# A new order table for the first token block, four scalings moved from GpSimd to VectorE, weight fetches split in halves

## The chip, the core and the metric

The kernel runs on one core of a Trainium2 chip. TensorE (PE) multiplies matrices, VectorE (DVE), ScalarE (ACT) and GpSimd (POOL) work on tiles, SyncE (SP) issues most DMA transfers. Each engine takes its instructions in program order and waits on semaphores for the others. The metric is the device time of one execution in microseconds. Lower is better.

## The reference

Three stages follow one another on 3072 tokens (4 batches of 768) of 512 channels:

```python
state = gamma * state + k[t] (x) v[t];  y[t] = scale * q[t] @ state      # retention, 8 heads of 64, per batch
g = max(0.01 * h, h), h = x @ w_in;     x2 = g @ w_out                   # w_in 512x2048, w_out 2048x512
e = argmax(x2 @ w_gate);  out = gate * (relu(x2 @ w1[e]) @ w2[e])        # 8 experts, 512x1024 and 1024x512
```

`w_in` and `w_out` come as 64-bit floats, everything else as 32-bit floats. Products are made to nearly 32-bit precision out of three products of high and low parts (`hi`, `lo`).

## The kernel before

**Work.** Retention works in chunks of 128 tokens, the second stage in 8 blocks of 384 tokens (3 chunks). For a block, `mm1(i, f)` makes hidden slice f (0 to 15) from 12 matmuls; ScalarE and VectorE make g and its parts from it (`t` and `gh` on ScalarE, `max` and `gl` on VectorE); `mm2(i, f)` adds the slice's share to the block's output with 9 matmuls. The experts come last.

**Block 0** is unlike the others: while it runs, the weights of the second stage arrive and are converted, and chunks 0 to 5 of the retention are computed. Its order is written out by hand in the string `FIRST`. Every word is a step, and each engine meets its own steps in the order of the string:

- `w n` (line 129, SP): two DMAs of 512 KB, one for each half of weight fetch n, into a ring of raw buffers. Fetch n uses the buffers of fetch n-4, so each half waits until the `L` step of that half of fetch n-4 has read them. `w-1` and `w15` have one half.
- `D`, `A`, `H` (ScalarE, lines 160, 156, 179) and `B`, `C`, `L` (VectorE, lines 162, 167, 181) with `n.m`: conversion of half m of fetch n, in the order D and A, B, C, H, L. B and C put sign, exponent and mantissa together, C reading what B wrote; H makes the high part, L the low part. `n.0` is the slice of `w_in` that `mm1` of f = n+1 needs (`-1.0` for f = 0), `n.1` the slice of `w_out` that `mm2` of f = n needs.
- `kv n` loads chunk n; `q n` and `k n` (lines 217 and 223) multiply its queries and keys by decay factors, on VectorE or GpSimd; `S`, `mask`, `ya`, `yb`, `U`, `st` are its scores (PE), masking (VectorE), outputs (PE), state product (PE) and state; `xh n` (ScalarE) and `xl n` (VectorE) make the high and low part of its output, the input of `mm1`.
- `mm1_f` and `mm2_f` are the matmuls of slice f. `masks` builds the mask on GpSimd.

Before, GpSimd scales the queries of chunks 1 and 6 and on, and the keys of chunks 0, 1 and 6 and on; VectorE scales the queries of chunks 0 and 2 to 5 and the keys of chunks 2 to 4 (the queries of chunk 0 by way of its output). Chunk 5's keys are not scaled. Chunk 6, the first of block 2, is loaded at the word `st5` and scaled at the word `xl5`. Chunk 0's inputs are loaded in two halves, ahead of the first word of the string. `KW` adds a few matmuls on zeros behind some words.

Of the kernel before, what the change touches and what calls it, by code (L numbers as in the profile page):

```python
# [13 lines left out]
U32 = mybir.dt.uint32  # L14
# [5 lines left out]
B, H, S, D = 4, 8, 768, 64  # L20
# [30 lines left out]
S1 = 1  # L51
S2 = 0
# [2 lines left out]
AC = (4, 8, 12)  # L55
KW = {"S0": 2, "U0": 1, "S1": 2, "S2": 2}
FIRST = """
w-1 kv1 kv2 w0 w1 w2 S0 masks D-1.0 A-1.0 mask00 mask01 k0 B-1.0 yb0 C-1.0 U0 H-1.0 y0 st1 xh0 q1 xl0 L-1.0 w3 k1 S1 U1 mask10 mask11 ya1 st2 D0.0 yb1
q2 A0.0 k2 S2 D0.1 B0.0 xh1 C0.0 A0.1 mask20 D1.0 mask21 ya2 H0.0 xl1 A1.0 yb2 L0.0 D1.1 B0.1 A1.1 C0.1 xh2 B1.1 D2.0 H0.1 xl2 A2.0 C1.1 mm1_0 D2.1
B1.0 H1.1 C1.0 A2.1 B2.0 mm1_1 t0 L0.1 w4 kv3 H1.0 max0 A3.0 L1.1 U2 gh0 C2.0 A3.1 gl0 D4.0 L1.0 w5 t1 B2.1 H2.0 mm2_0 max1 D3.0 L2.0 gh1 D4.1 C2.1  # L60
A4.1 gl1 mm1_2 B3.0 H2.1 C3.0 D3.1 A4.0 L2.1 w6 kv4 mm2_1 t2 B3.1 H3.0 max2 D5.0 q3 gh2 L3.0 A5.0 mm1_3 gl2 D5.1 C3.1 st3 B4.0 C4.0 mm2_2 B5.0 H3.1
C5.0 t3 L3.1 w7 A6.0 mm1_4 max3 H5.0 B4.1 gh3 C4.1 D6.1 S3 gl3 H4.0 L5.0 H4.1 L4.0 t4 mm2_3 D6.0 mask31 A5.1 max4 D7.0 mask30 gh4 L4.1 w8 mm1_5 A7.1
gl4 A6.1 B5.1 A7.0 C5.1 t5 B7.0 mm2_4 H5.1 max5 A8.0 B6.1 gh5 L5.1 w9 D8.0 mm1_6 gl5 D8.1 C7.0 A8.1 q4 D9.0 B6.0 t6 mm2_5 H7.0 C6.0 A9.0 max6 L7.0
H6.0 ya3 k3 A9.1 yb3 L6.0 D9.1 gh6 C6.1 U3 kv5 D7.1 gl6 H6.1 B8.0 mm1_7 xh3 B7.1 st4 L6.1 w10 C8.0 C7.1 mm2_6 t7 xl3 H7.1 max7 H8.0 L7.1 w11 gh7 mm1_8
L8.0 gl7 B8.1 S4 A10.0 C8.1 t8 B9.0 D10.0 max8 H8.1 mask41 mm2_7 gh8 L8.1 w12 D10.1 C9.0 D11.0 A10.1 gl8 mm1_9 mask40 H9.0 B9.1 A11.1 L9.0 D11.1 C9.1
t9 mm2_8 A12.0 max9 H9.1 k4 gh9 B10.1 A12.1 gl9 mm1_10 D12.1 L9.1 w13 D12.0 C10.1 A13.0 B10.0 H10.1 mm2_9 C10.0 t10 B11.1 H10.0 C11.1 ya4 D13.0 max10
A11.0 yb4 L10.0 gh10 B11.0 A13.1 U4 C11.0 xh4 H11.1 gl10 mm1_11 q5 H11.0 L10.1 w14 w15 D13.1 st5 L11.0 L11.1 mm2_10 B12.0 t11 C12.0 A14.0 max11 H12.0
xl4 mm1_12 gh11 L12.0 D14.1 gl11 S5 A14.1 B13.0 t12 C13.0 D15.0 max12 A15.0 B12.1 mm2_11 gh12 C12.1 D14.0 gl12 H12.1 B13.1 mm1_13 C13.1 L12.1 H13.0
mask50 H13.1 L13.0 t13 mm2_12 max13 L13.1 gh13 mask51 gl13 mm1_14 B14.1 B14.0 t14 C14.0 mm2_13 max14 H14.0 C14.1 gh14 L14.0 H14.1 ya5 B15.0 yb5 L14.1
C15.0 xh5 gl14 mm1_15 H15.0 xl5 L15.0 t15 mm2_14 max15 gh15 gl15  # L70
"""


# [1 line left out]
def tile_retention_moe_moe(  # L75
# [12 lines left out]
    nc = tc.nc  # L88
# [26 lines left out]
    raws = {}  # L115

    def whalf(slot, h, dtype, nm):
        return wp.tile([128, 1024], dtype, tag=f"W{slot}{'ab'[h]}", name=nm)
# [7 lines left out]
    def pieces(n):  # L126
        return [(0, n + 1), (1, n)] if 0 <= n < 15 else [(0, 0)] if n < 0 else [(1, 15)]

    def w_fetch(n):
        if n in (-1, 15):  # L130
            t = [whalf(12, 0, U32, "raw") if n < 0 else stg.tile([128, 1024], U32, tag="stg", name="stg")]
        else:
            s, h = 12 + 2 * (n % 2 == 0), int(n % 4 in (1, 2))
            t = [whalf(s + x, h, U32, "raw") for x in range(2)]
        raws[n] = t
        for x in range(len(t)):
            nc.sync.dma_start(out=t[x][:, :512 * (2 if wide else 1)], in_=w[n + 1, :, x].bitcast(U32))

    def conv(o, n, m):
        x, f = pieces(n)[m]  # L140
        conv_op(o, n, m, x, f)
# [53 lines left out]
    def attn_load(n):  # L195
        b, cc = divmod(n, 2 * NC)
        if n == 2:

            t = [whalf(8, h, F32, "kv") for h in range(2)]
            parts = [t[x // 2][:, x % 2 * 512:x % 2 * 512 + 512] for x in range(4)]  # L200
            for h in range(2):
                nc.sync.dma_start(out=t[h], in_=qkv[b, cc, :, h * 1024:(h + 1) * 1024])
        else:
            t = at.tile([128, 2048], F32, tag="kv", name="kv")
            parts = [t[:, x * 512:x * 512 + 512] for x in range(4)]
            if n == 0:
                nc.sync.dma_start(out=t[:, :1024], in_=qkv[b, cc, :, :1024])
                nc.scalar.dma_start(out=small, in_=c_m[:, :200])
                nc.scalar.dma_start(out=qd, in_=c_m[:, 200:])
                nc.sync.dma_start(out=t[:, 1024:], in_=qkv[b, cc, :, 1024:])  # L210
            else:
                nc.sync.dma_start(out=t, in_=qkv[b, cc])
        loads[n] = parts

    def attn_q(n):
        q = loads[n][0]
        (nc.vector if n in (0, 2, 3, 4, 5) else nc.gpsimd).tensor_mul(q, q, qd)

    def attn_k(n):
        cc = n % (2 * NC)  # L220
        if cc < 5:
            k = loads[n][2].rearrange("p (g d) -> p g d", d=64)
            (nc.vector if n in (2, 3, 4) else nc.gpsimd).tensor_mul(k, k, kd[:, cc].unsqueeze(2).to_broadcast([128, 8, 64]))

    def pairs():
        return [(j, h, slice(64 * h, 64 * h + 64), slice(j * 128 + 64 * h, j * 128 + 64 * h + 64), slice(j * 128, (j + 1) * 128))
# [557 lines left out]
    raw = {}  # L784
# [8 lines left out]
    for x in ORDER:  # L793
        k = sum(y[0] == x for y in items)
# [408 lines left out]
    with tc.manual_schedule():  # L1203
# [22 lines left out]
        def first(word, o, n, m):  # L1226
            if o in ("A", "B", "C", "D", "H", "L"):
                conv(o, n, m)
            elif o == "w":
                w_fetch(n)  # L1230
            elif o == "kv":
                attn_load(n)
            elif o == "masks":
                masks()
            elif o == "q":
                attn_q(n)
            elif o == "k":
                attn_k(n)
            elif o == "S":
                banks[n] = attn_scores(n, tag_s.get(n, ("m0", "m1")))  # L1240
            elif o == "mask":
                ams[n, m] = attn_mask(n, banks[n][m], m)
            elif o == "ya":
                ys[n] = attn_yq(n, tag_y.get(n, ("m0", "m1")))
            elif o == "yb":
                ys[n] = attn_y(n, [ams[n, h] for h in range(2)], ys.get(n))
            elif o == "y":
                y0 = early["y"].rearrange("p (j t) -> p j t", j=4)
                nc.vector.tensor_mul(y0[:, :2], ys[n][0][0][:, :2], qd.rearrange("p (j t) -> p j t", j=4)[:, :2])
                nc.vector.tensor_mul(y0[:, 2:], ys[n][0][0][:, 2:], early["qy"])  # L1250
                ys[n] = [(y0, slice(0, 4))]
            elif o == "U":
                attn_U(n)
            elif o == "st":
                attn_state(n)
            elif o == "xh":
                attn_xh(n, ys[n])
            elif o == "xl":
                attn_xl(n, ys[n])
            elif o == "mm1":  # L1260
                banks["h", n] = mm1(0, n)
            elif o == "t":
                h = banks["h", n]
                gs[n] = gp.tile([128, TB], F32, tag="t", bufs=1, name="t")
                nc.scalar.activation(out=gs[n], in_=h, func=ACTF.Copy, scale=0.01)
            elif o == "max":
                nc.vector.tensor_max(gs[n], gs[n], banks["h", n])
            elif o == "gh":
                ghi = gp.tile([128, TB], F32R, tag="gh", name="gh")
                nc.scalar.copy(out=ghi, in_=gs[n])  # L1270
                gs[n] = gs[n], ghi
            elif o == "gl":
                act_b(0, n, *gs[n])
# [174 lines left out]
```

## Time and profile before

| | |
|---|---|
| device time, median of 3 runs | 988.24 us (987.54 to 989.04) |
| profiled execution | 989.41 us, its span 987.4 us |
| PE busy | 968.1 us, 98% |
| VectorE busy | 526.9 us, 53% |
| ScalarE busy | 422.4 us, 43% |
| GpSimd busy | 157.6 us, 16% |

The span runs from the first to the last instruction in the trace. Times in the rows are microseconds from its start. A timeline row gives start and duration, engine and line, what is written from what, and in brackets how long the engine had been idle and what it had waited for. A start-to-start distance of two rows of one engine is the price of the first in a full queue; durations of neighbours overlap a little.

### The profile page before, as it was taken

How to read it: one execution, taken by the hardware profiler on the slowest of the kernel's cores; microseconds unless marked ns; L12 is line 12 of the kernel's file. 1: busy time of each engine (PE TensorE's matmuls, PEld its weight loads, DVE VectorE, ACT ScalarE, POOL GpSimd, SP SyncE). 2: the span in 40 equal slices, each digit the busy share in tenths (PEclk: the TensorE clock that was granted, in tenths of full speed). 3: DMA queues.
4: the chain of work that ended last, by engine and by line, in shares of the span. 5: the costliest groups of instructions: out<-in, count | busy, mean ns of one | idle time of the engine just before them, and what ended most of it. 6: DMA issues, size and time to landing. Idle time of an engine off the chain costs nothing.

```text
span 987.4 us, 16775 instructions
## 1 busy us (share of the span) xinstructions
PE 968.1 (98%) x6513; PEld 843.4 (85%) x6513; DVE 526.9 (53%) x1092; ACT 422.4 (43%) x771; POOL 157.6 (16%) x131
## 2 busy tenths in 40 slices
PE   7998999999999999999999999999999999999996
PEld 6887888988888888888888888888988887887985
DVE  5999544434443443444444357555754655755741
ACT  4986332223222232222222233533655656655741
POOL 2001021021012010111102000633211321222111
PEclk9999999999999999999999999999999999999999
DMA  8773222323323213213413012312037968967600
GB/s 342 271 252 133 85 59 60 91 60 59 88 63 59 60 47 104 60 33 79 99 33 76 18 33 90 103 33 76 27 104 283 292 256 326 318 221 253 205 24 31
DMA packets 75105, 121.06 MB, mean 123 GB/s; under 512 B 36108, under 2 KB 36494, under 8 KB 72208
## 3 DMA queue, kind: packets, MB, share of 16 engines
q1 hardware_dynamic: 70352, 105.96, 34.5%
q0 software_dynamic: 4384, 13.65, 4.0%
q8 instruction: 51, 0.84, 0.4%
q10 hardware_dynamic: 288, 0.36, 0.1%
q14 instruction: 30, 0.25, 0.1%
HBM read 117.06 MB, written 13.25 MB: 132 GB/s over the span
## 4 chain that ended last, share of the span: by engine, by line
PE 73%; issue 10%; DMA 6%; DVE 5%; ACT 3%; POOL 2%; POOLq 0%; ACTq 0%; SPq 0%
PE x L371 25%; PE h L331 24%; PE m L932 6%; PE m L957 6%; DMA out_dram<-mq,sidx 3%; DMA raw<-in_w_dram 3%; PE ay L237 2%; PE y L281 2%; PE m L988 1%; PE m L1016 1%; PE y L272 1%; PE xt L893 1%; ACT raw L160 1%; PE m L1029 1%; DVE wl L181 1%
## 5 line engine op out<-in xcount | busy, mean ns | idle before, releaser
L350 DVE TENSOR_TENSOR t<-t,h 128x384 f32<-128x384 f32 x111 | 61.2, 552 | 158.3 <-ACT t L349 158.3
L862 DVE TENSOR_TENSOR wu<-raw,wu 128x1024 fp32r<-128x1024 f32 x96 | 114.0, 1222 | 47.6 <-ACT wu L861 46.4
L932 PE MATMUL m<-xe,wu 128*128 128x256 f32 x1056 | 137.6, 284 | 0.1
L932 PEld LDWEIGHTS m<-xe,wu 128*128 128x128 f32 x1056 | 132.3, 191 | 3.2 <-issue 0.5
L358 DVE TENSOR_TENSOR gl<-t,gh 128x384 fp32r<-128x384 f32 x127 | 80.4, 633 | 94.2 <-ACT gh L351 93.5
L349 ACT ACTIVATE t<-h 128x384 f32<-128x384 f32 x111 | 54.4, 490 | 155.9 <-PE h L331 125.6
L371 PE MATMUL x<-wh,gl 128*128 128x512 f32 x288 | 116.1, 403 | 1.8 <-DVE gl L358 1.8
L371 PE MATMUL x<-wl,gh 128*128 128x512 f32 x288 | 113.2, 393 | 1.4 <-DVE wl L181 1.4
L371 PE MATMUL x<-wh,gh 128*128 128x512 f32 x288 | 112.7, 391 | 0.0
L351 ACT CAST gh<-t 128x384 fp32r<-128x384 f32 x111 | 57.0, 514 | 128.0 <-PE x L371 71.2
L957 PE MATMUL m<-wu,gh 128*128 128x512 f32 x352 | 109.2, 391 | 0.0
L861 ACT CAST wu<-raw 128x1024 fp32r<-128x1024 f32 x104 | 104.5, 1047 | 3.0 <-DMA raw<-in_w_dram 3.0
L331 PE MATMUL h<-xh,wl 128*128 128x384 f32 x384 | 85.9, 345 | 0.8 <-ACT xh L292 0.7
L478 POOL TENSOR_TENSOR xr<-xr,b 128x512 f32<-128x512 f32 x18 | 20.9, 1164 | 398.4 <-DVE gl L358 231.8
L331 PE MATMUL h<-xl,wh 128*128 128x384 f32 x384 | 82.7, 336 | 0.2 <-DVE xl L298 0.2
L331 PE MATMUL h<-xh,wh 128*128 128x384 f32 x384 | 82.1, 334 | 0.0
L957 PEld LDWEIGHTS m<-wu,gh 128*128 128x128 f32 x352 | 66.3, 188 | 12.4
L331 PEld LDWEIGHTS h<-xh,wl 128*128 128x128 f32 x384 | 66.5, 188 | 5.1 <-ACT xh L292 1.0
L957 PE MATMUL m<-wu,gl 128*128 128x512 f32 x176 | 70.2, 399 | 0.4 <-DVE gl L944 0.3
L331 PEld LDWEIGHTS h<-xl,wh 128*128 128x128 f32 x384 | 68.9, 188 | 0.5 <-DVE xl L298 0.5
L331 PEld LDWEIGHTS h<-xh,wh 128*128 128x128 f32 x384 | 67.9, 188 | 0.0
L371 PEld LDWEIGHTS x<-wh,gl 128*128 128x128 f32 x288 | 54.0, 188 | 14.7 <-DVE gl L358 2.5
(267 smaller groups left out, 1462.3 us busy)
## 6 DMA issues: line engine op xcount, KB each, us to landing
raw<-in_w_dram SPq DMA_DIRECT2D x159, 512.0 KB
kv<-in_qkv_dram SPq DMA_DIRECT2D x22, 1024.0 KB
x2d<-xr SPq DMA_DIRECT2D x24, 256.0 KB
kv<-in_qkv_dram SPq DMA_DIRECT2D x4, 512.0 KB
t<-b SPq DMA_TRANSPOSE x36
stg<-in_w_dram SPq DMA_DIRECT2D x1, 512.0 KB
mq<-in_cm_dram ACTq DMA_DIRECT2D x1, 256.0 KB
kv<-x2d,gidx POOLq DMA_INDIRECT x16, 4.4
```

Of the source, the lines that this page charges most:

```text
L237: nc.tensor.matmul(banks[h][:, js], kt[r, js], q[r, js], start=True, stop=True, skip_group_check=True)
L331: nc.tensor.matmul(h, wcols(a, fc * 512 + k * 128, 128), x[:, k, :], start=(n == 0), stop=(n == 11))
L349: nc.scalar.activation(out=t, in_=h, func=ACTF.Copy, scale=0.01)
L350: nc.vector.tensor_max(g, t, h)
L351: nc.scalar.copy(out=ghi, in_=g)
L358: nc.vector.tensor_sub(glo, g, ghi.bitcast(F32))
L371: nc.tensor.matmul(x2ps[i][t], a[:, ts], wcols(w, f % 4 * 512), start=(f == 0 and n == 0), stop=(f == 15 and n == 2))
L478: (nc.gpsimd if S1 else nc.vector).tensor_sub(x, x, b1)
L861: nc.scalar.copy(out=hi, in_=src)
L862: (nc.gpsimd if g == 0 else nc.vector).tensor_sub(lo, src, hi.bitcast(F32))
L932: nc.tensor.matmul(bank, wp_[k // 2][a][:, c:c + 128], x[:, k, :], start=(n == 0), stop=(n == 11))
L957: nc.tensor.matmul(m2ps[2 * q + h], a[:, ts], w[:, fs], start=(f == 0 and n == 0), stop=(f == 7 and n == 2))
```

## The change

Three things are in the diff. The string `FIRST` is a new order of the same steps, with the fetches 4 to 14 (apart from 8) written as two words, one for each half, and `w_fetch` issues the halves that the word names. The queries and keys of chunks 1 and 6 are scaled by VectorE. Chunk 6 is scaled at the word `gl15`, the last of the string, and no longer at `xl5`. The description of the change also names the first weights as moved ahead of the second half of chunk 0's inputs; no line of the diff does this, `attn_load(0)` still issues both halves ahead of the string.

```diff
@@ -55,19 +55,19 @@
 AC = (4, 8, 12)
 KW = {"S0": 2, "U0": 1, "S1": 2, "S2": 2}
 FIRST = """
-w-1 kv1 kv2 w0 w1 w2 S0 masks D-1.0 A-1.0 mask00 mask01 k0 B-1.0 yb0 C-1.0 U0 H-1.0 y0 st1 xh0 q1 xl0 L-1.0 w3 k1 S1 U1 mask10 mask11 ya1 st2 D0.0 yb1
-q2 A0.0 k2 S2 D0.1 B0.0 xh1 C0.0 A0.1 mask20 D1.0 mask21 ya2 H0.0 xl1 A1.0 yb2 L0.0 D1.1 B0.1 A1.1 C0.1 xh2 B1.1 D2.0 H0.1 xl2 A2.0 C1.1 mm1_0 D2.1
-B1.0 H1.1 C1.0 A2.1 B2.0 mm1_1 t0 L0.1 w4 kv3 H1.0 max0 A3.0 L1.1 U2 gh0 C2.0 A3.1 gl0 D4.0 L1.0 w5 t1 B2.1 H2.0 mm2_0 max1 D3.0 L2.0 gh1 D4.1 C2.1
-A4.1 gl1 mm1_2 B3.0 H2.1 C3.0 D3.1 A4.0 L2.1 w6 kv4 mm2_1 t2 B3.1 H3.0 max2 D5.0 q3 gh2 L3.0 A5.0 mm1_3 gl2 D5.1 C3.1 st3 B4.0 C4.0 mm2_2 B5.0 H3.1
-C5.0 t3 L3.1 w7 A6.0 mm1_4 max3 H5.0 B4.1 gh3 C4.1 D6.1 S3 gl3 H4.0 L5.0 H4.1 L4.0 t4 mm2_3 D6.0 mask31 A5.1 max4 D7.0 mask30 gh4 L4.1 w8 mm1_5 A7.1
-gl4 A6.1 B5.1 A7.0 C5.1 t5 B7.0 mm2_4 H5.1 max5 A8.0 B6.1 gh5 L5.1 w9 D8.0 mm1_6 gl5 D8.1 C7.0 A8.1 q4 D9.0 B6.0 t6 mm2_5 H7.0 C6.0 A9.0 max6 L7.0
-H6.0 ya3 k3 A9.1 yb3 L6.0 D9.1 gh6 C6.1 U3 kv5 D7.1 gl6 H6.1 B8.0 mm1_7 xh3 B7.1 st4 L6.1 w10 C8.0 C7.1 mm2_6 t7 xl3 H7.1 max7 H8.0 L7.1 w11 gh7 mm1_8
-L8.0 gl7 B8.1 S4 A10.0 C8.1 t8 B9.0 D10.0 max8 H8.1 mask41 mm2_7 gh8 L8.1 w12 D10.1 C9.0 D11.0 A10.1 gl8 mm1_9 mask40 H9.0 B9.1 A11.1 L9.0 D11.1 C9.1
-t9 mm2_8 A12.0 max9 H9.1 k4 gh9 B10.1 A12.1 gl9 mm1_10 D12.1 L9.1 w13 D12.0 C10.1 A13.0 B10.0 H10.1 mm2_9 C10.0 t10 B11.1 H10.0 C11.1 ya4 D13.0 max10
-A11.0 yb4 L10.0 gh10 B11.0 A13.1 U4 C11.0 xh4 H11.1 gl10 mm1_11 q5 H11.0 L10.1 w14 w15 D13.1 st5 L11.0 L11.1 mm2_10 B12.0 t11 C12.0 A14.0 max11 H12.0
-xl4 mm1_12 gh11 L12.0 D14.1 gl11 S5 A14.1 B13.0 t12 C13.0 D15.0 max12 A15.0 B12.1 mm2_11 gh12 C12.1 D14.0 gl12 H12.1 B13.1 mm1_13 C13.1 L12.1 H13.0
-mask50 H13.1 L13.0 t13 mm2_12 max13 L13.1 gh13 mask51 gl13 mm1_14 B14.1 B14.0 t14 C14.0 mm2_13 max14 H14.0 C14.1 gh14 L14.0 H14.1 ya5 B15.0 yb5 L14.1
-C15.0 xh5 gl14 mm1_15 H15.0 xl5 L15.0 t15 mm2_14 max15 gh15 gl15
+w-1 kv1 kv2 w0 w1 w2 S0 masks D-1.0 A-1.0 mask01 k0 mask00 yb0 B-1.0 C-1.0 U0 y0 H-1.0 q1 xh0 st1 S1 L-1.0 w3 k1 mask11 U1 mask10 D0.0 st2 ya1 q2 A0.0
+yb1 xl0 D0.1 B0.0 A0.1 S2 k2 xh1 C0.0 D1.0 mask20 A1.0 mask21 H0.0 D1.1 xl1 ya2 A1.1 L0.0 w4.0 yb2 A2.0 B0.1 D2.0 B1.0 xh2 C0.1 A2.1 xl2 H0.1 C1.0 mm1_0
+D3.0 L0.1 w4.1 kv3 H1.0 B1.1 A3.1 L1.0 w5.0 t0 mm1_1 A3.0 max0 D4.0 C1.1 gh0 B2.0 U2 H1.1 gl0 D2.1 C2.0 t1 L1.1 w5.1 H2.0 mm2_0 max1 A4.1 B2.1 gh1 B3.0
+D4.1 C2.1 D3.1 mm1_2 A4.0 gl1 q3 H2.1 C3.0 t2 D5.0 mm2_1 L2.0 w6.0 H3.0 max2 A5.1 L2.1 w6.1 kv4 gh2 L3.0 w7.0 D5.1 mm1_3 gl2 st3 B3.1 A5.0 B4.1 t3 C3.1
+mm2_2 D6.0 C4.1 A6.0 max3 H4.1 B4.0 gh3 mm1_4 L4.1 D6.1 gl3 H3.1 C4.0 A6.1 S3 L3.1 w7.1 H4.0 B5.0 t4 A7.0 L4.0 w8 mm2_3 D7.0 max4 C5.0 gh4 mask30 H5.0
+gl4 mm1_5 L5.0 w9.0 D7.1 mask31 A7.1 B5.1 t5 D8.0 mm2_4 B6.0 A8.0 max5 D8.1 C5.1 gh5 C6.0 H5.1 mm1_6 gl5 D9.0 L5.1 w9.1 A9.0 k3 A8.1 B6.1 mm2_5 H6.0 q4
+t6 L6.0 ya3 C6.1 yb3 max6 H6.1 B7.0 gh6 U3 kv5 w10.0 L6.1 w10.1 A9.1 xh3 gl6 mm1_7 C7.0 st4 xl3 H7.0 B7.1 D9.1 L7.0 w11.0 t7 mm2_6 B8.0 max7 C8.0 gh7
+C7.1 mm1_8 H8.0 gl7 H7.1 L8.0 A10.0 S4 L7.1 w11.1 w12.0 t8 D10.0 B8.1 A10.1 B9.0 mm2_7 D10.1 C8.1 D11.0 C9.0 H8.1 max8 H9.0 mask41 mm1_9 gh8 L8.1 w12.1
+D11.1 gl8 A11.0 L9.0 w13.0 t9 B9.1 A11.1 mm2_8 max9 D12.0 C9.1 gh9 mask40 A12.0 H9.1 gl9 mm1_10 B10.1 A12.1 L9.1 w13.1 D12.1 C10.1 t10 D13.0 mm2_9 B10.0
+H10.1 B11.0 A13.0 C10.0 ya4 C11.0 yb4 H10.0 k4 A13.1 L10.0 w14.0 U4 xh4 max10 D13.1 L10.1 w14.1 w15 gh10 mm1_11 B11.1 st5 gl10 C11.1 t11 q5 H11.0 mm2_10
+B13.1 H11.1 L11.0 D14.0 xl4 A14.0 D14.1 max11 mm1_12 B13.0 A14.1 gh11 B12.0 D15.0 S5 gl11 A15.0 C12.0 t12 L11.1 H12.0 max12 mm2_11 L12.0 gh12 B12.1 gl12
+C12.1 mm1_13 C13.0 H12.1 C13.1 t13 L12.1 H13.0 max13 mm2_12 H13.1 L13.0 gh13 L13.1 gl13 B14.1 mm1_14 mask50 mask51 t14 B14.0 mm2_13 max14 C14.0 gh14
+C14.1 ya5 H14.0 gl14 yb5 H14.1 L14.0 L14.1 xh5 B15.0 mm1_15 xl5 C15.0 t15 H15.0 mm2_14 max15 L15.0 gh15 gl15
 """
 
 
@@ -126,14 +126,16 @@
     def pieces(n):
         return [(0, n + 1), (1, n)] if 0 <= n < 15 else [(0, 0)] if n < 0 else [(1, 15)]
 
-    def w_fetch(n):
+    def w_fetch(n, halves):
         if n in (-1, 15):
             t = [whalf(12, 0, U32, "raw") if n < 0 else stg.tile([128, 1024], U32, tag="stg", name="stg")]
         else:
             s, h = 12 + 2 * (n % 2 == 0), int(n % 4 in (1, 2))
-            t = [whalf(s + x, h, U32, "raw") for x in range(2)]
+            t = raws.get(n, [None] * 2)
+            for x in halves:
+                t[x] = whalf(s + x, h, U32, "raw")
         raws[n] = t
-        for x in range(len(t)):
+        for x in halves[:len(t)]:
             nc.sync.dma_start(out=t[x][:, :512 * (2 if wide else 1)], in_=w[n + 1, :, x].bitcast(U32))
 
     def conv(o, n, m):
@@ -214,13 +216,13 @@
 
     def attn_q(n):
         q = loads[n][0]
-        (nc.vector if n in (0, 2, 3, 4, 5) else nc.gpsimd).tensor_mul(q, q, qd)
+        (nc.vector if n in (0, 1, 2, 3, 4, 5, 6) else nc.gpsimd).tensor_mul(q, q, qd)
 
     def attn_k(n):
         cc = n % (2 * NC)
         if cc < 5:
             k = loads[n][2].rearrange("p (g d) -> p g d", d=64)
-            (nc.vector if n in (2, 3, 4) else nc.gpsimd).tensor_mul(k, k, kd[:, cc].unsqueeze(2).to_broadcast([128, 8, 64]))
+            (nc.vector if n in (1, 2, 3, 4, 6) else nc.gpsimd).tensor_mul(k, k, kd[:, cc].unsqueeze(2).to_broadcast([128, 8, 64]))
 
     def pairs():
         return [(j, h, slice(64 * h, 64 * h + 64), slice(j * 128 + 64 * h, j * 128 + 64 * h + 64), slice(j * 128, (j + 1) * 128))
@@ -1227,7 +1229,7 @@
             if o in ("A", "B", "C", "D", "H", "L"):
                 conv(o, n, m)
             elif o == "w":
-                w_fetch(n)
+                w_fetch(n, [m] if "." in word else [0, 1])
             elif o == "kv":
                 attn_load(n)
             elif o == "masks":
@@ -1280,6 +1282,7 @@
                 attn_load(6)
             elif word == "xl5":
                 attn_load(7)
+            elif word == "gl15":
                 attn_q(6)
                 attn_k(6)
             elif word == "mm1_8":
```

## Rows read from the trace of the kernel before

**Rows 1.** The page, busy time and share of the span by engine
```profile
PE 968.1 (98%) x6513; PEld 843.4 (85%) x6513; DVE 526.9 (53%) x1092; ACT 422.4 (43%) x771; POOL 157.6 (16%) x131
```

**Rows 2.** Stretches: length, then busy us of each engine, granted clock, DMA share, GB/s
```profile
30.00:40.00 10.00, 9.36 (x46) 8.45 (x47) 9.93 (x19) 9.77 (x22) 0.00 (x0) 1.00 1.00 366
...
90.00:100.00 10.00, 7.90 (x33) 6.92 (x32) 9.70 (x14) 2.83 (x6) 3.23 (x2) 0.83 0.00 0
```

**Rows 3.** PE's waits, 0 to 130 us: total, times, longest
```profile
PE x L371 <- DVE w L181: 2.1, 1, 2.1
...
PE x L371 <- DVE gl L358: 1.5, 2, 1.2
PE x L371 <- DVE wl L181: 1.4, 2, 0.8
```

**Rows 4.** The chain that ended last, 48 to 111 us: start, duration, what
```profile
48.26 4.75 DMA raw<-in_w_dram
...
82.46 3.83 DMA raw<-in_w_dram
...
94.56 3.10 PE x L371 x8
97.66 2.69 PE h L331 x12
...
106.36 2.08 PE x L371 x9
108.44 2.10 PE h L331 x12
```

**Rows 5.** A finer stretch, columns as in rows 2
```profile
97.00:98.00 1.00, 1.00 (x4) 0.88 (x3) 1.00 (x3) 0.00 (x0) 0.00 (x0) 0.50 0.00 0
```

**Rows 6.** VectorE's timeline where its queue is full
```profile
24.56 0.75 DVE L298 TENSOR_TENSOR xl<-y,xh 128x256 fp32r<-128x256 f32 x2
...
25.83 0.69 DVE L162 SCALAR_TENSOR_TENSOR raw<-raw 128x512 uint32<-128x512 uint32 x1
26.55 0.69 DVE L167 SCALAR_TENSOR_TENSOR raw<-raw 128x512 uint32<-128x512 uint32 x1
...
27.76 0.68 DVE L181 TENSOR_TENSOR wl<-raw,wh 128x512 fp32r<-128x512 f32 x1
28.36 0.55 DVE L1267 TENSOR_TENSOR t<-t,h 128x384 f32<-128x384 f32 x1
28.83 0.69 DVE L181 TENSOR_TENSOR wl<-raw,wh 128x512 fp32r<-128x512 f32 x1
```

**Rows 7.** VectorE's timeline, three instructions beside GpSimd's
```profile
14.14 1.37 DVE L298 TENSOR_TENSOR xl<-early,xh 128x512 fp32r<-128x512 f32 x1 [0.35 <-ACT xh L292]
...
91.39 1.66 DVE L167 SCALAR_TENSOR_TENSOR val<-raw 128x512 uint32<-128x512 uint32 x1
92.98 1.53 DVE L181 TENSOR_TENSOR w<-val,w 128x512 fp32r<-128x512 f32 x1
```

**Rows 8.** GpSimd's timeline, 0 to 150 us
```profile
13.92 1.04 POOL L223 TENSOR_TENSOR kv<-kv,mq 128x512 f32<-128x512 f32 x1
...
90.72 1.78 POOL L217 TENSOR_TENSOR kv<-kv,mq 128x512 f32<-128x512 f32 x1 [75.76 <-DMA kv<-in_qkv_dram]
92.47 1.49 POOL L223 TENSOR_TENSOR kv<-kv,mq 128x512 f32<-128x512 f32 x1
```

**Rows 9.** ScalarE's timeline, from fetch 1's landing to chunk 2's output
```profile
20.67 0.68 ACT L160 ACTIVATE raw<-raw 128x512 uint32<-128x512 uint8 x1 [0.59 <-DMA raw<-in_w_dram]
...
23.51 0.62 ACT L292 CAST xh<-y 128x256 fp32r<-128x256 f32 x2
```

**Rows 10.** PE's timeline, the first matmuls of block 0
```profile
23.91 0.97 PE L331 MATMUL h<-xh,wl 128*128 128x384 f32 x4 [0.72 <-ACT xh L292]
```

**Rows 11.** ScalarE's waits, 24 to 95 us: total, times, longest
```profile
ACT raw L156 <- DMA raw<-in_w_dram: 1.4, 2, 0.9
ACT raw L160 <- DMA raw<-in_w_dram: 1.0, 2, 0.7
```

## Prediction

> **What bounds the kernel now.** I read the page first: PE is busy for 98% of the span [rows 1]. From the table of stretches onwards, what is left to win lies almost wholly in block 0: VectorE is busy 9.93 us of the ten from 30 to 40, ScalarE 9.77 [rows 2], and PE waits for VectorE there. The list of PE's waits names three sources of size, 2.1 + 1.5 + 1.4 = 5.0 us, all on VectorE's `L` or `gl` [rows 3]. The longest is one wait of 2.1 us, and behind it the chain view holds PE alone: from 94.56 on, nothing but matmuls, so what PE gains in block 0 it keeps to the end. The 8 matmuls behind that wait take 3.10 us where 9 take 2.08 later, the next `mm1` takes 2.69 against 2.10 [rows 4]. The granted clock explains it: 0.50 from 97 to 98, that is 1.2 instead of 2.4 GHz, after the wait [rows 5]. Loss by the clock: 3.10 - 8/9 x 2.08 = 1.25, and 0.59, together 1.84 us.
>
> The timeline of VectorE shows why the wait is there. The instruction that PE waits for is `L12.1`, at 92.98; it takes 1.53 us, the `C13.1` ahead of it 1.66 [rows 7], where such instructions have 0.69 and 0.68 [rows 6]. In just this stretch GpSimd scales chunk 6, from 90.72 to 94 [rows 8]. The two instructions lost (1.66 - 0.69) + (1.53 - 0.68) = 1.82 us.
>
> **VectorE's queue, part by part.** I count what VectorE does from the end of `xl2` (next start 24.56 + 0.67 = 25.23) to the end of `L12.1` (94.43 by start-to-start price). Both strings have 113 instructions there, the same kinds: 85 on 128x512 tiles, 26 `max` and `gl`, 2 `xl`. Prices from start to start: 0.60 for a 128x512 one (27.76 to 28.36), 0.47 for `max` or `gl` (28.36 to 28.83), 0.67 for `xl` (2 instructions) [rows 6]. With 0.605 and 0.467 before rounding, 51.4 + 12.1 + 1.3 = 64.8 us.
>
> *Pairs.* A `C` right behind its own `B` starts 0.72 us after it (25.83 to 26.55), 0.12 more than the 0.60 [rows 6]. In the old string 15 such pairs stand in this stretch, in the new none: 15 x 0.12 = 1.8 us are removed. The Trainium skill (VectorE: DVE Perf Modes, section "The DRAIN you can't avoid") states that VectorE's chained instructions take as long with a semaphore after each as with one at the end. By that the pairs would cost nothing and the sum would come out 1.8 us later; the row differs, and I go by the row.
>
> *GpSimd's neighbours.* Scaling chunk 6 at `gl15` on VectorE takes 1.82 us out of this stretch. It adds 2 x 0.60 us behind the last `gl`, where PE has two `mm1` of 2.10 us of block 1 to do before it needs anything later from VectorE: hidden. If that cover failed it would cost 1.2 us.
>
> *The rest.* 94.43 - 25.23 = 69.20; 69.20 - 64.8 - 1.8 - 1.82 = 0.8 us are short waits and rounding. For the new string I take twice that, 1.6, since in the first 20 us of the stretch, up to `gl4`, ScalarE has 40 steps in both strings, and VectorE 40 in the old but 38 in the new: ScalarE, hardly less full there [rows 2], loses the little lead it had, and each will wait for the other more. Bounds: 0.8, and what the ring rival below gives. New length 64.8 + 1.6 = 66.4 us.
>
> **The start.** `q1` and `k1` join VectorE's queue, 2 x 0.60 = 1.2 us; `xl0`, which took 1.37 us beside GpSimd's `k1` [rows 7, 8], falls to 0.68, and two pairs are parted, 0.24. VectorE thus comes to `xl2` at 24.56 + 1.2 - 0.69 - 0.24 = 24.8. The scores of chunk 1 can start earlier, but that gains nothing: ScalarE waits until 20.67 for the landing of fetch 1 all the same, which the change does not move [rows 9]. From that landing to `xh2` the old string has five ScalarE steps, (23.51 - 20.67) / 5 = 0.57 us each; the new has seven (`A2.0` and `D2.0` now stand ahead of `xh2`). So `xh2` starts at 20.67 + 7 x 0.57 = 24.65, 1.1 later. PE's first `mm1` began 0.40 after `xh2` [rows 9, 10]: now 25.05. `xl2` can't start sooner either: its end moves from 25.23 to 25.05 + 0.67 = 25.72. This is a cost of 0.5 us for VectorE and 1.1 for PE.
>
> The split fetches cost SP the same DMAs, two per fetch; each half already waited for its own `L` alone, so the words only change what stands between on SP's queue (`kv3`, `kv4`, `kv5`): nothing, with the ring rival as the bound. Weights ahead of chunk 0's second half are not in the diff: nothing; were they, the landing of fetch 1, behind the same bytes, would still set 20.67.
>
> **The sum.** `L12.1` is done at 25.72 + 66.4 = 92.1, against 94.43. PE then had 108.44 - 94.56 = 13.88 us to the end of block 0, 1.84 of them lost to the clock: 12.04 without. With the same 0.13 between: 92.1 + 0.13 + 12.04 = 104.3, against 108.44. Gain 4.1 us, of which VectorE's queue brings 2.3 and the clock 1.8. The best case is PE alone: 108.44 - 23.91 - 5.0 - 1.84 = 77.7 us of work [rows 3, 4, 10], from 25.05 to 102.75, a gain of 5.7. The span of 987.4 becomes 983.3, and 2.0 us lie around it (989.41 in the profiled execution, 1.2 above the median). On the median: 988.24 - 4.1 = 984.1 us.
>
> **The rivals.**
>
> *The clock falls all the same.* By the sum PE, 1.1 late and without stalls on the way, would come to `mm2_12` at 94.56 - 2.1 - (1.5 + 1.4) + 1.1 = 90.7 and find `L12.1` 1.4 us away; and ahead of the first `mm1` the wait of 0.72 grows to some 1.9. For it: after 2.1 us the clock did fall. Against it: after the wait of 1.2 us near 30 [rows 3] it stayed at 1.00 [rows 2], and VectorE's lateness will come in several shorter waits (the `L11.1` of the `mm2` before is due by the same prices only 0.4 us less late). The Trainium skill (TensorE: Matmul & The Clock Gate, section "HAM oscillation — how this bites in real kernels") has matmuls behind a long wait for data start at the lower clock; the trace agrees at 97 us. Price 1.84 again: gain 2.3, 985.9 us.
>
> *The pairs cost nothing*, because what follows a parted pair waits as long for something else. Gain 4.1 - 1.8 = 2.3: 985.9 us. The rule on chained instructions above would make it so; the row of 0.72 speaks against it.
>
> *The ring is too short (slower).* A fetch lands 3.83 to 4.75 us after the `L` that freed its buffer [rows 4]. By VectorE's prices 11 of the 22 halves of fetches 4 to 14 now have less than 4.75 us between that `L` and their first ScalarE step, several 4.0; in the old string six had. ScalarE waited 1.4 + 1.0 = 2.4 us for fetches [rows 11], and hardly any of it reached VectorE. If all 11 wait and pass it on in full, it decides against the change from 6.1 / 11 = 0.55 us each (the gain and 0.2%); at 4.75 - 4.0 = 0.75 each it costs 8.3: 992.4 us. At 0.37 each it eats the gain: 988.2, no change.
>
> **How the numbers follow.** A measurement of this kernel can tell about 0.2%, 2.0 us, from no change. Chances: the sum as it stands, 984.1, 0.53; PE alone as the bound, 982.5, 0.10; the clock falls again, 985.9, 0.15; the pairs cost nothing, 985.9, 0.05; the ring eats the gain, about 988.2, 0.10; the ring makes it slower, 992.4, 0.07. Faster is the first four, 0.83; same 0.10; slower 0.07. The range from 982.4 to 986.6 leaves out the two ring cases (0.17) and little else.
>
> **What would show it.** Right: `C13.1` and `L12.1` at 0.69; no `C` 0.72 behind its own `B`; GpSimd idle from its `k0` to block 1; `xh2` near 24.7 and the first `mm1` near 25.1; `L12.1` done near 92; block 0 over near 104.3; clock 1.00 through 90 to 100. Wrong: VectorE idle in pieces behind ScalarE's waits for fetches, a granted clock under 1 anywhere from 25 to 100, the first `mm1` well behind 25.1, or a new wait of PE after block 0.

## The result, and the profile after

The changed kernel took **993.01 us** (median of 7 runs, 990.80 to 995.73) beside 987.54 for the kernel before on the same chip (median of 7, 984.76 to 990.20): ratio **1.0061**, 95% interval 1.0045 to 1.0077. It became slower; the forecast was 984.1 us, range 982.4 to 986.6. The profiled execution took 995.73 us, its span 993.9; it is the longest of the seven, so stages and waits read from it may be larger than in the median run. Lines of the changed file stand two lower than in the kernel before (`L181` is now `L183`, `L160` `L162`, `L156` `L158`, `L331` `L333`).

The busy times of the profile's page answer to [rows 1]: VectorE and ScalarE do the same work, GpSimd 5.4 us less, and the span has grown by 6.5 us.

```profile
PE 970.0 (98%) x6513; PEld 843.3 (85%) x6513; DVE 526.4 (53%) x1096; ACT 422.3 (42%) x771; POOL 152.2 (15%) x127
```

All of it arises in block 0. Its first matmul starts at 23.81 (23.91 before), block 1's first at 114.78 (108.28 before):

```profile
23.81 0.97 PE L333 MATMUL h<-xh,wl 128*128 128x384 f32 x4 [1.58 <-ACT xh L294]
...
114.78 0.87 PE L333 MATMUL h<-xh,wl 128*128 128x384 f32 x4
```

The stage is thus 90.97 us long instead of 84.37, 6.6 more. The table of stretches (columns as in [rows 2]) shows who lost:

```profile
30.00:40.00 10.00, 9.66 (x48) 8.18 (x47) 8.97 (x17) 8.85 (x20) 0.00 (x0) 1.00 0.69 252
40.00:50.00 10.00, 8.01 (x42) 6.42 (x41) 7.42 (x13) 6.70 (x13) 0.00 (x0) 0.83 0.76 268
...
70.00:80.00 10.00, 8.92 (x43) 7.23 (x41) 8.56 (x16) 8.44 (x17) 0.00 (x0) 1.00 0.67 230
90.00:100.00 10.00, 7.24 (x35) 5.54 (x34) 7.18 (x13) 4.76 (x9) 0.00 (x0) 0.71 0.42 169
```

VectorE, busy for at least 9.66 us of every ten from 30 to 100 before, is busy for 7.18 to 8.97 us of these; it is still full only from 60 to 70 and from 80 to 90. It now waits for ScalarE, and ScalarE for weights. ScalarE's waits from 24 to 100 (total, times, longest):

```profile
ACT raw L162 <- DMA raw<-in_w_dram: 9.0, 6, 2.7
ACT raw L158 <- DMA raw<-in_w_dram: 1.9, 3, 1.1
ACT w L181 <- DVE val L169: 1.8, 1, 1.8
ACT gh L1272 <- DVE t L1269: 1.4, 2, 1.1
ACT wh L181 <- DVE raw L169: 1.1, 1, 1.1
```

That is 9.0 + 1.9 = **10.9 us in front of fetches that had not landed**, 2.4 before [rows 11]. VectorE's waits in the same stretch add up to 9.7 us, 8.7 of them for ScalarE:

```profile
DVE gl L360 <- ACT gh L1272: 5.1, 3, 2.8
DVE wl L183 <- ACT wh L181: 2.0, 1, 2.0
DVE t L1269 <- ACT t L1267: 1.6, 2, 1.4
DVE kv L219 <- DMA kv<-in_qkv_dram: 1.0, 1, 1.0
```

How one wait becomes another is seen in the chain of work that ended last, from 84 us on (start, duration, what):

```profile
84.69 0.61 DVE wl L183
...
85.33 7.00 DMA raw<-in_w_dram
...
92.35 0.67 ACT raw L162
93.01 0.54 ACT raw L158
93.55 0.41 ACT gh L1272
...
93.98 0.56 DVE gl L360
...
95.89 3.75 PE x L373 x8
99.64 2.79 PE h L333 x12
```

`L10.1` frees the buffer at 85.3, the second half of fetch 14 takes 7.00 us to land, and ScalarE, standing at `D14.1`, can't go on to `gh11`, whose input had long been there. VectorE then waits 2.82 us at `gl11`, PE 2.26 us. Behind that wait the granted clock is 0.50 (1.2 of 2.4 GHz) from 95 to 101: PE's next 8 matmuls take 3.75 us and the `mm1` behind them 2.79.

### The profile page after: what moved, and what is told of

Read it like the earlier page. It is cut to its first block, busy times and chain, and to the rows that moved or that the text cites. A ratio compares the mean times of both kernels' runs of the same rounds, so it can differ in the third digit from the quotient of the medians.

```text
span 993.9 us, 16773 instructions
## 1 busy us (share of the span) xinstructions
PE 970.0 (98%) x6513; PEld 843.3 (85%) x6513; DVE 526.4 (53%) x1096; ACT 422.3 (42%) x771; POOL 152.2 (15%) x127
## 4 chain that ended last, share of the span: by engine, by line
PE 72%; issue 10%; DMA 8%; DVE 5%; ACT 2%; POOL 2%; POOLq 0%; SPq 0%; ACTq 0%
PE x L373 24%; PE h L333 24%; PE m L934 6%; PE m L959 6%; DMA raw<-in_w_dram 5%; DMA out_dram<-mq,sidx 3%; PE ay L239 2%; PE y L283 2%; PE m L990 1%; PE m L1018 1%; PE y L274 1%; PE xt L895 1%; DVE wl L183 1%; PE m L1031 1%; PE u L253 1%
## 5 line engine op out<-in xcount | busy, mean ns | idle before, releaser
L333 PE MATMUL h<-xh,wl 128*128 128x384 f32 x384 | 86.1, 345 | 1.9 <-ACT xh L294 1.6
L333 PE MATMUL h<-xl,wh 128*128 128x384 f32 x384 | 82.5, 336 | 0.0
L333 PE MATMUL h<-xh,wh 128*128 128x384 f32 x384 | 82.1, 334 | 0.0
L333 PEld LDWEIGHTS h<-xh,wl 128*128 128x128 f32 x384 | 66.5, 188 | 6.6 <-ACT xh L294 1.8
L333 PEld LDWEIGHTS h<-xl,wh 128*128 128x128 f32 x384 | 68.9, 188 | 0.0
L333 PEld LDWEIGHTS h<-xh,wh 128*128 128x128 f32 x384 | 67.9, 188 | 0.0
```

The source lines that it names most:

```text
L333: nc.tensor.matmul(h, wcols(a, fc * 512 + k * 128, 128), x[:, k, :], start=(n == 0), stop=(n == 11))
```

## The experiments

Each was timed in 5 rounds beside the kernel before on the same chip, the two kernels with chunk 6 loaded late in 3, the short chunks once. "Fetch waits" are ScalarE's for weights from 24 to 100 us, "VectorE waits" those of its `H` and `gh` steps for VectorE's `raw`, `val` and `t` there, in one profile of each kernel. A stage runs from the first matmul of block 0 to that of block 1. The expectations quote other windows: from 10 to 112 us ScalarE waited 14.3 us for fetches in the changed kernel, as it stands at fetches ahead of block 0 too.

| kernel | ratio to before, 95% | stage | fetch waits | VectorE waits |
|---|---|---|---|---|
| before | 1 | 84.37 | 2.4 | 7.1 |
| changed | 1.0061 (1.0045 to 1.0077) | 90.97 | 10.9 | 4.3 |
| 1: old table, new scalings | **0.9976** (0.9966 to 0.9987) | 81.14 | 1.7 | 6.1 |
| 2: new table, old scalings | 1.0072 (1.0051 to 1.0093) | 89.14 | 9.0 | 6.3 |
| 3: changed + buffers | 1.0011 (1.0000 to 1.0023) | 83.39 | 6.3 | 4.0 |
| 4: changed, short chunks | 992.59 us once | 87.43 | 8.2 | 3.8 |
| 5: as 1, pairs parted | 0.9980 (0.9970 to 0.9989) | 80.50 | 2.1 | 8.1 |
| 6: as 5 + buffers | 0.9977 (0.9968 to 0.9987) | 80.38 | 2.1 | 8.0 |
| 7: changed, chunk 6 late | 1.0042 (1.0028 to 1.0056) | 87.68 | 9.4 | 4.2 |
| 8: as 7 + buffers | 1.0001 (0.9987 to 1.0015) | 83.31 | 5.8 | 4.5 |
| 9: changed, lead 4 | 1.0048 (1.0031 to 1.0065) | 86.00 | none | 13.7 |
| 10: as 9 + buffers | 1.0026 (1.0014 to 1.0038) | 86.06 | none | 13.2 |
| 11: changed, lead 8 | 1.0011 (1.0002 to 1.0020) | 84.15 | 0.5 | 7.7 |
| 12: as 11 + buffers | 0.9997 (0.9988 to 1.0006) | 81.96 | 0.5 | 7.2 |

**1 and 2: the two halves of the change.** Experiment 1 is the kernel before with the diff's edits of `attn_q`, `attn_k` and `gl15`; experiment 2 is the changed kernel without them.

> The old order with the four scalings alone moved to VectorE, chunk 6 scaled at gl15. Both theories let the old fetch distances stand. Theory 1 (the new order asks for fetches before they can land, the scalings help): GpSimd is idle in block 0, C13.1 and L12.1 take 0.69 us each, the wait of 2.1 us in front of mm2_12 falls under 0.6 and the clock stays at 1.00: 2 to 3.6 us faster than before, ratio 0.9965 to 0.998. Theory 2 (the scalings on VectorE make the change slow, by filling the queue that bounds block 0): slower than before, ratio 1.002 to 1.006.

> The new order and split fetches with the scalings on GpSimd as before, chunk 6 scaled at xl5. Theory 1: still slower than before by about what the change was, ratio 1.004 to 1.009, with ScalarE's waits for fetches between 10 and 16 us in block 0. Theory 2: near before, 0.998 to 1.002.

The scalings alone give 0.9976, the new table alone 1.0072: both as theory 1 had it. The loss lies in the new table, the scalings are a gain. VectorE's timeline of experiment 1 answers to [rows 7]: beside an idle GpSimd, `C13.1` and `L12.1` take 0.69 and 0.68 us.

```profile
90.15 0.69 DVE L167 SCALAR_TENSOR_TENSOR val<-raw 128x512 uint32<-128x512 uint32 x1
90.76 0.68 DVE L181 TENSOR_TENSOR w<-val,w 128x512 fp32r<-128x512 f32 x1
```

PE waits 0.2 us for that `w` instead of 2.1 [rows 3], and the clock stays up:

```profile
30.00:40.00 10.00, 10.00 (x51) 8.92 (x50) 9.93 (x18) 10.00 (x22) 0.00 (x0) 1.00 1.00 369
90.00:100.00 10.00, 9.75 (x72) 8.02 (x71) 9.93 (x18) 4.63 (x10) 0.00 (x0) 1.00 0.00 1
```

From the end of `xl2` to the end of `L12.1` it needs 91.36 - 24.20 = 67.16 us, 2.04 less than the 69.20 of before, where 1.82 was forecast for this part. The Trainium skill (SBUF — State Buffer, section "Who interferes with whom") has a VectorE instruction with two inputs in SBUF contend with a GpSimd instruction that reads SBUF. The trace agrees; [rows 7, 8] show both sides lengthened, `C13.1` to 1.66 us beside a GpSimd scaling of 1.78, where one of the same shape in the changed kernel takes 1.30 at 134 us.

**3 and 4: why the fetches come late.** Experiment 3 gives fetches 4 to 6 fresh buffers, so that they wait for no `L`:

```diff
-                t[x] = whalf(s + x, h, U32, "raw")
+                t[x] = whalf(5 + n, x, U32, "raw") if n in (4, 5, 6) else whalf(s + x, h, U32, "raw")
```

> The changed kernel, but fetches 4, 5 and 6 land in weight buffers that stand empty by then (slots 9, 10, 11), so that fetches 4 to 6 and 8 to 10 wait for no L. Theory 1: ScalarE's waits for fetches fall from 14.3 us to under 7, block 0 ends at least 3 us before the 114.8 us of the changed kernel, ratio to before 0.996 to 1.003. Theory 3 (the loss is PE's late start and the low clock by themselves): ratio stays 1.004 to 1.008.

Experiment 4 leaves out all but the queries of chunks 3 to 6 (zeros stand in their place), so that each such load moves a quarter of its bytes:

```diff
-                nc.sync.dma_start(out=t, in_=qkv[b, cc])
+                if 3 <= n <= 6:
+                    nc.sync.dma_start(out=t[:, :512], in_=qkv[b, cc, :, :512])
+                    nc.gpsimd.memset(t[:, 512:], 0.0)
+                else:
+                    nc.sync.dma_start(out=t, in_=qkv[b, cc])
```

> The changed kernel with a quarter of the bytes in the loads of chunks 3 to 6: keys and values of these chunks are left out (set to zero by GpSimd), so only block 0 is read from it. Theory 1a (a fetch lands late because the 1 MB loads of chunks stand between or beside the halves): the trips of 5.5 to 8.4 us fall to 4 to 5.5, ScalarE's waits for fetches fall under 8 us of 14.3, block 0 ends 2 us or more before 114.8. Theory 1b (the distance alone is too short, whatever else is under way): the waits stay over 11 us.

The buffers recover 0.5% and take 4.6 of the 10.9 us of fetch waits away: the wait for a free buffer is a cause. They took away less than expected: from 10 to 112 us ScalarE still waited 9.6 us, not under 7. The run also changes what is under way beside later fetches, since SP no longer waits there for `L` steps: chunks 3 and 4 are loaded at 19.3 and 25.6 us instead of 26.3 and 38.0.

The short chunks decide little. They take 2.7 us of fetch waits away, and block 0 ends 3.3 us sooner (111.44), as theory 1a had it; but the trips on the chain still take 5.1 to 7.8 us, not 4 to 5.5, and the waits from 10 to 112 us are 11.7, as theory 1b had it. The one time of 992.59 us lies within those of the changed kernel. That the chunks' bytes lengthen the trips is not shown by it.

**5 and 6: what the pairs are worth.** In the old table with the new scalings, 18 `B`/`C` pairs of block 0 are parted by a VectorE step from close by; one line of it:

```diff
-C5.0 t3 L3.1 w7 A6.0 mm1_4 max3 H5.0 B4.1 gh3 C4.1 D6.1 S3 gl3 H4.0 L5.0 H4.1 L4.0 t4 mm2_3 D6.0 mask31 A5.1 max4 D7.0 mask30 gh4 L4.1 w8 mm1_5 A7.1
+C5.0 t3 L3.1 w7 A6.0 mm1_4 max3 H5.0 B4.1 gh3 gl3 C4.1 D6.1 S3 H4.0 L5.0 H4.1 L4.0 t4 mm2_3 D6.0 mask31 A5.1 max4 D7.0 mask30 gh4 L4.1 w8 mm1_5 A7.1
```

> The old order with the scalings on VectorE (ratio 0.9976 by itself) and one thing more: in each of the 18 pairs a neighbouring VectorE step of the old order stands between B and its C. If a pair costs 0.12 us as the prediction has it, VectorE's stretch from xl2 to L12.1 is 1.8 us shorter, and block 0 ends 1 to 1.8 us before 103.6 (less where PE is bound by itself): ratio 0.9955 to 0.9968. If a parted pair gives nothing, because the step waits for something else: 0.997 to 0.9985.

> The same with fetches 4, 5 and 6 in slots 9, 10 and 11, empty by then, so that six fetches wait for no L. The fetch theory expects little, since ScalarE waits only 1.7 us for fetches in the old order: within 0.001 of the ratio without it. If waits for fetches were hidden behind VectorE's full queue, now shorter: 0.001 to 0.002 better.

15 of the 18 pairs stand in VectorE's stretch, so 15 x 0.12 = 1.8 us should have come out of it. It shrank by 0.5 (66.66), and that is not the pairs' doing: one edit puts `C13.1` behind `L12.1` and so takes an instruction of 0.60 us out of the stretch. With `C13.1` counted it is 67.3 us long, as in experiment 1. The time didn't fall either: 0.9980 beside 0.9976, each inside the other's interval. ScalarE's waits for VectorE grew from 6.1 to 8.1 us, since `C` and `L` now come later, and VectorE's own waits for ScalarE grew with them (0.4 to 1.5 us). The parted pair starts sooner and what follows it waits. Ahead of block 0 the edit may have cost time: `mask20` now stands between `B0.0` and `C0.0`, where VectorE waits 1.02 us for the scores of chunk 2, and the first matmul started at 24.59 and 24.42 in the two profiles, at 22.50 in experiment 1. So the time alone would not settle it; the stretch does. Buffers add nothing here, as this table hardly waits for fetches.

**7 and 8: chunk 6's load.** In the changed kernel its 1 MB was issued within 2 us of the fetches 14 and 15. Here ScalarE issues it later, at `H14.1`:

```diff
-                nc.sync.dma_start(out=t, in_=qkv[b, cc])
+                (nc.scalar if n == 6 else nc.sync).dma_start(out=t, in_=qkv[b, cc])
...
-            elif word == "st5":
+            elif word == "H14.1":
```

> The changed kernel with the load of chunk 6 (1 MB) taken off SP's queue behind fetch 15 and issued by ScalarE behind H14.1. If a fetch lands late because of the bytes under way beside it: the second half of fetch 14, 7.0 us from its L to landing, takes 4.5 to 5.5, ScalarE's wait of 2.7 us for it falls under 1.2, PE's clock stays up near 95, and block 0 ends 2 to 4 us before 114.8. If the trip is set by something else it stays at 6.5 or more and block 0 ends where it did, within 1 us.

> The changed kernel with both the three empty slots for fetches 4 to 6 and the late load of chunk 6. The fetch theory: the gains add, ScalarE's waits for fetches fall from 6.0 to under 4, block 0 ends at 104 to 106, ratio to before 0.996 to 1.000. If the rest of the loss is the order itself (steps of ScalarE and VectorE that wait for one another): block 0 still ends after 106.3.

The trip of `w14.1` fell from 7.00 to 5.65 us, ScalarE's wait there from 2.66 to 1.52:

```profile
84.12 5.65 DMA raw<-in_w_dram
```

That is the way that was expected, but not as far: 4.5 to 5.5 and under 1.2 us were expected, and a granted clock that stays up, which fell to 0.50 again at 94. Time 1.0042 instead of 1.0061, with intervals that overlap; beside the buffers the step is 1.0001 against 1.0011, which overlap too. There the gains did not add: the fetch waits stayed at 5.8 us where under 4 were expected, and block 0 ended at 107.54, later than the 106.3 from which on the expectation blames the order itself.

The Trainium skill (DMA: Bandwidth & Descriptors, section "Issuing engines are not separate DMA queues") has transfers of all issuers share the same 16 engines and interleave; the shorter trip with less under way agrees. It is not the whole of it: in the kernel before, the same half `w14.1` was issued at 82.46 with fetch 15 and chunk 6 as close behind it as in the changed kernel, and took 3.83 us [rows 4].

```profile
82.84 0.42 SPq L137 DMA_DIRECT2D stg<-in_w_dram  x1
83.36 0.38 SPq L212 DMA_DIRECT2D kv<-in_qkv_dram  x1
```

In the changed kernel it was issued at 85.33, and they at:

```profile
85.70 0.42 SPq L139 DMA_DIRECT2D stg<-in_w_dram  x1
86.22 0.38 SPq L214 DMA_DIRECT2D kv<-in_qkv_dram  x1
```

What differs is ahead of it: `w14.0` was issued 1.1 us before `w14.1`, in experiment 7 too, and 3.3 us before it in the old table. No run changes that alone, so why the trip was long stays open.

**9 to 12: where ScalarE takes its first steps.** If ScalarE stands in front of fetches because `D` and `A` stand too early in the table, moving those alone should help. In experiments 9 and 10 the `D` and `A` of fetches 4 to 15 were moved to four VectorE steps ahead of their `B`, if they stood earlier; in 11 and 12 to eight. In the changed table they stand 5 to 25 VectorE steps ahead. The order of VectorE's, PE's and SP's steps and of ScalarE's others stays. Two lines of experiment 11:

```diff
-t6 L6.0 ya3 C6.1 yb3 max6 H6.1 B7.0 gh6 U3 kv5 w10.0 L6.1 w10.1 A9.1 xh3 gl6 mm1_7 C7.0 st4 xl3 H7.0 B7.1 D9.1 L7.0 w11.0 t7 mm2_6 B8.0 max7 C8.0 gh7
-C7.1 mm1_8 H8.0 gl7 H7.1 L8.0 A10.0 S4 L7.1 w11.1 w12.0 t8 D10.0 B8.1 A10.1 B9.0 mm2_7 D10.1 C8.1 D11.0 C9.0 H8.1 max8 H9.0 mask41 mm1_9 gh8 L8.1 w12.1
+C6.1 yb3 D8.0 A8.0 max6 H6.1 B7.0 gh6 U3 kv5 w10.0 L6.1 w10.1 xh3 gl6 mm1_7 C7.0 st4 xl3 H7.0 B7.1 D8.1 A8.1 L7.0 w11.0 t7 mm2_6 D9.0 A9.0 B8.0 max7
+C8.0 gh7 C7.1 mm1_8 H8.0 gl7 H7.1 L8.0 S4 L7.1 w11.1 w12.0 t8 B8.1 A9.1 D9.1 B9.0 mm2_7 C8.1 C9.0 H8.1 max8 H9.0 mask41 mm1_9 gh8 A10.1 D10.1 L8.1
```

> The changed kernel with one thing moved in its order: for fetches 4 to 15 ScalarE's D and A stand four VectorE steps ahead of the B that needs them, and not earlier; the orders of VectorE, PE and of the fetches are those of the changed kernel. By VectorE's prices 21 of the 22 ring halves then have 9 us or more from the L that frees their buffer to their first step (before the move 11 had under 4.75). Theory 1 (the changed kernel is slow because ScalarE meets a fetch before it has landed and stands there with everything behind it): ScalarE's waits for fetches in block 0 fall from 14.3 us to under 4, block 0 ends 5 to 9 us before 114.8, ratio to before 0.996 to 1.001. Theory 4 (the order of VectorE's and PE's steps is at fault, or VectorE lacks the lead that ScalarE had won): ratio 1.004 or more, whatever the waits for fetches.

> The same with fetches 4 to 6 in slots 9 to 11. Theory 1: nothing left to win by it, within 0.001 of the run without it. If fetches still set the time: 0.002 or more better.

> The changed kernel with the A and D steps of fetches 4 to 15 written eight VectorE steps ahead of their B instead of wherever the new table put them (the lead was four VectorE steps in the run before, 9 to 17 us behind the freeing L by prices; now 8 to 17, A13.1 3.6). Theory 1 (ScalarE stands only in front of unlanded fetches, and the four-step lead was too small a cushion for the handshakes): fetch waits stay under 3 us and ScalarE's waits for VectorE fall from 14 us to under 6; time 0.997 to 1.001 of before. Theory 4 (the rest of the loss lies in the new table's order of B, C, H, L and max, gl steps, whatever the lead of A and D): handshake waits stay about 10 us or more, time 1.003 to 1.006.

> The run beside it, with fetches 4, 5 and 6 in buffers of their own as well, so that fetches 4 to 10 are waited for less. Theory 1: within 0.1% of the run beside it, since that one hardly waits for fetches, and 0.997 to 1.0005 of before. Theory 4: 1.002 to 1.005, handshake waits as in the run beside it.

With a lead of four no fetch of the stage is waited for, but the kernel gains little: 1.0048, where theory 1 had 0.996 to 1.001 and theory 4 1.004 or more. So it is not enough to take the fetch waits away. ScalarE's waits of experiment 9, same view and stretch as above:

```profile
ACT wh L181 <- DVE raw L169: 6.7, 6, 2.2
ACT gh L1272 <- DVE t L1269: 5.2, 5, 1.5
ACT w L181 <- DVE val L169: 1.8, 1, 1.8
```

ScalarE now idles for VectorE before the step that VectorE needs next, and VectorE waits 4.1 us for `wh` in turn. Buffers gained 0.22% here, where no fetch was waited for and under 0.1% was expected; the intervals overlap, the two stages are as long, and the record doesn't explain it. With a lead of eight both are small (experiment 11):

```profile
ACT wh L181 <- DVE raw L169: 4.8, 5, 1.3
ACT gh L1272 <- DVE t L1269: 2.2, 3, 1.6
ACT w L181 <- DVE val L169: 0.7, 1, 0.7
ACT raw L158 <- DMA raw<-in_w_dram: 0.5, 1, 0.5
```

Fetch waits of 0.5 us and VectorE waits of 7.7, about the 7.1 of before: 1.0011, and 0.9997 with the buffers. So 0.50 of the 0.85% that lie between the changed kernel and experiment 1 come back by where `D` and `A` stand. The buffers alone had given back as much (experiment 3); on top of the lead of eight they give another 0.14, with intervals that overlap. Two different edits, one that lets fetches start sooner and one that has ScalarE come to them later, thus recover the same part. Neither expectation held whole: the times lie at the edge of what the theory of early first steps gave (0.997 to 1.001) and inside it, but the waits for VectorE did not fall under 6 us, and the two runs differ by 0.14%, not 0.1.

**What stays open.** Experiment 12 is still 0.2% behind experiment 1, which has the same scalings and the old table; its stage is 0.8 us longer, and its block 0 started 1.5 us later. In it VectorE still waits 2.6 us for ScalarE's `w`, which experiment 1 does not show. Whether the rest is the new table's order of `B`, `C`, `H` and `L`, the fetches split in halves, which every run of the new table has, or its start (ScalarE's seven steps ahead of `xh2`), no run parts: the start of block 0 lay between 22.50 and 24.59 us in the profiles with the old table, and between 23.36 and 24.23 in those with the new one. A ring of more than four fetches throughout was not tried. **The best version is experiment 1, 0.24% faster than before; experiments 5 and 6 can't be told from it.**

## Why the prediction was wrong, point by point

**The scalings: right.** `C13.1` and `L12.1` fell to 0.69 us, GpSimd stands idle from 8.8 to 133 us, and in experiment 1 VectorE's stretch lost 2.04 us where the forecast had 1.82, with the clock at 1.00 throughout. The rival that the clock falls again did not come true there. On the median, though, experiment 1 gained 2.3 us, not 1.82 + 1.84. Of the 23 runs of the kernel before beside it, 12 had a mean granted clock of 0.996 and a median of 988.0 us, the other 11 a higher one and 986.2. That suggests that the clock was lost in about half of its runs; the forecast read the loss from one profile and took it off the median whole.

**The start: right but for fetch 1.** In the changed kernel ScalarE's wait for fetch 1 ended at 19.40, not 20.67. Why is not shown; it ended at 19.23 in experiment 1, with the old table, and at 20.63 in experiment 9, with the new one, so it goes with neither table. That the first matmul came 1.2 us sooner than forecast is luck. From there the seven steps took what was forecast: 19.40 + 7 x 0.57 = 23.39, and `xh2` started at 23.35.

```profile
19.40 0.69 ACT L162 ACTIVATE raw<-raw 128x512 uint32<-128x512 uint8 x1 [1.03 <-DMA raw<-in_w_dram]
...
23.35 0.68 ACT L294 CAST xh<-y 128x256 fp32r<-128x256 f32 x2
```

**"The rest": the step that failed.** The prediction put 1.6 us on all that VectorE would wait for, between a bound of 0.8 and the ring rival, as if ScalarE's waits for fetches would go on not reaching VectorE. From the end of `xl2` (24.46) to that of `L12.1` (99.61 + 0.60) the changed kernel took 75.75 us, so the term measured 75.75 - 64.8 = **10.9 us**, 8.7 of them waits for ScalarE. (That ScalarE's fetch waits come to 10.9 too is chance.) Its excess is 9.3 of the 10.6 us by which block 0 ended later than forecast: 114.94 in the chain view, in which the forecast was reckoned, against 104.3. The sign that the prediction had named came true: VectorE idle in pieces behind ScalarE's waits for fetches. Twice the residue of before was no estimate of it: the residue came from a table whose waits for fetches hardly reached VectorE.

**The clock: lost again, elsewhere.** From the end of `L12.1` to the end of block 0 it took 114.94 - 100.21 = 14.73 us, 12.17 forecast: 2.6 more. PE did not wait for `L12.1` at all; it was still at the matmuls ahead of `mm2_12`, which began at 102.3. The 8 matmuls at a clock of 0.50 took 3.75 us and the `mm1` 2.79; by the prices of [rows 4] at a clock of 1.00, 8/9 x 2.08 and 2.10, they lost 2.6 us. The start, earlier than forecast, gives 1.3 back: 9.3 + 2.6 - 1.3 = 10.6.

**The ring rival had the mechanism, and 0.07.** It put 8.3 us on 11 waits of 0.75 and 992.4 us on the kernel; measured were 9 waits of 1.2, 10.9 us, and 993.01. That the two times are so near is in part luck: the rival had the waits pass on in full, VectorE waited 8.7 us for ScalarE, and the clock cost 2.6 us that the rival did not have. Two readings kept its chance low. The trips of 3.83 to 4.75 us [rows 4] were taken as the length of any trip, yet they are those of one profile's chain (experiment 1, with the same table, has one of 5.70). In the changed kernel's chain they are longer:

```profile
27.32 8.36 DMA raw<-in_w_dram
...
37.53 7.19 DMA raw<-in_w_dram
...
47.89 6.24 DMA raw<-in_w_dram
...
69.34 5.55 DMA raw<-in_w_dram
```

And "hardly any of it reached VectorE" was read from a table where ScalarE's steps behind the waiting ones were not urgent. In the new one they are the `gh` and `wh` that VectorE takes next. That the prediction counted ScalarE's lead as a number of steps (40 against VectorE's 40 and 38) and not by which step stands behind which fetch is what hid this.

**The pairs: the price was right, the gain nothing.** A `B` and its own `C` stand 0.72 us apart, and parting them does not shorten VectorE's stretch (experiment 5): for this term the sum of that rival, 985.9 us, was right, and so was its reason, that what follows waits as long. The Trainium skill's rule on chained instructions (VectorE: DVE Perf Modes, section "The DRAIN you can't avoid"), by which the pairs have no price, gives the same time, but for another reason; the row of 0.72 beside 0.60 still speaks against it as a rule on the instruction.

## What to carry to other kernels

On an engine that takes its instructions in order, a step that needs a prefetch is a wait placed in front of everything behind it: price it by what stands next on that engine and who needs that, and take the prefetch's length from a trip with the same transfers issued close to it, ahead of it too. A step's best place lies between two losses, too early (it waits for the transfer) and too late (its consumer waits for it): here four, eight and the table's own lead gave 1.0048, 1.0011 and 1.0061. A price per instruction that is saved inside a lockstep of two engines is no gain until a run shows it.

## What the runs showed of the hardware that was not expected

A 512 KB fetch took 3.5 to 8.4 us from its issue to its landing (3.51 in experiment 12, 8.36 in the changed kernel), in kernels that move the same bytes. Over the long trips of the changed kernel the DMA engines were busy for 0.79 to 0.86 of the time and moved less, not more, than the 366 GB/s at a share of 1.00 that the old table kept from 30 to 40 us [rows 2]; two of them, 28 to 36 and 85 to 92.5 us:

```profile
28.00:36.00 8.00, 7.27 (x48) 5.93 (x46) 6.97 (x13) 6.86 (x14) 0.00 (x0) 1.00 0.79 283
...
85.00:92.50 7.50, 7.24 (x47) 5.98 (x45) 6.16 (x12) 4.56 (x12) 0.00 (x0) 1.00 0.85 244
```

Why a trip of 7 us moves fewer bytes per us than a full stretch was not tried further.

The clock fell to 0.50 behind a wait of PE of 1.77 us as well (46 us), where waits of 1.2 us near 30 us of the kernel before [rows 2, 3], of 1.77 us at 84 us of experiment 12 and of 2.20 us at 56 us of experiment 7 left it at 1.00. In experiment 7 it then fell at 93, behind waits of 0.65 and 0.80. The length of a wait alone does not tell whether the clock will fall. The changed kernel behind 46 us:

```profile
47.00:48.00 1.00, 1.00 (x3) 0.81 (x3) 1.00 (x3) 0.44 (x2) 0.00 (x0) 0.50 0.36 139
```
